# Attention for one query: VectorE's products over K as one nested loop in place of two unrolled ones

## The chip, the cores and the metric

The kernel runs on one core of one Trainium2 chip. Its time is the device time of one execution in microseconds; the median of three runs is given. A profile, taken by the hardware profiler, is of one further execution. The engines are TensorE (PE), VectorE (DVE), ScalarE (ACT), GpSimd (POOL) and SyncE (SP); each has a sequencer of its own that reads the engine's instructions and hands them on (DVEq, ACTq and so on in the profile).

## What is computed

Sixteen heads of attention with a single query row each, over 8192 keys of 256 numbers in bfloat16:

```python
B, H, Sq, Sk, D = 1, 16, 1, 8192, 256
scale = q.shape[-1] ** -0.5
scores = jnp.einsum("bhqd,bhkd->bhqk", q, k) * scale
p = _softmax(scores, axis=-1)
return jnp.einsum("bhqk,bhkd->bhqd", p, v)
```

K and V are 67 MB each and are read once. Each key needs one product with the query and one with its weight, so there is little arithmetic for a byte.

## The kernel before, in words

The heads go in eight pairs. A pair's K (8.4 MB) lies on 128 partitions: 64 for each of its two heads, and on every partition 128 columns (J) of 256 numbers, one key each. V lies in the same way. K has two buffers (the halves of `kbuf`, `par` is the pair's parity), V one, `vbuf`.

SyncE issues all transfers, in the order of `ORDER` (line 17): k0 k1 v0 k2 v1 k3 and so on, with the last K and the last two Vs in pieces. Before K of pair n it waits until the products of pair n - 2 are done (lines 128 to 130): VectorE's share by the semaphore `kd`, GpSimd's by `tp`. Before V it waits until TensorE has used the former V (`pa`, `pr`).

A score is the sum of 256 products of a K column and the query. The 128 columns of a pair are shared out, each half of 64 (a side, `HJ`) apart:
- GpSimd multiplies columns 0 to 23 of the first side and 64 to 81 of the second, three at a time (line 218), and ScalarE adds these up (line 463).
- VectorE takes the others, 24 to 63 and 82 to 127: one `scalar_tensor_tensor` a column (line 262), which multiplies by the scale and the query and adds up into a column of `S`. That is 86 columns a pair, 688 in all.

VectorE's program is a loop over the pairs (line 245). At its start come the former pair's maximum (`top`, line 237), the maximum over partitions (`xmax`, line 241, with a step of TensorE before and after), and the reciprocal of a sum of an older pair. Then VectorE waits for the query and for K (`k_waits`) and runs two loops, one for each side: four times 10 columns for the first, two times 23 for the second (`CH`, line 15; lines 255 to 271). Each pass ends with an increment of `kd`; a pair makes `NC` = 6 of them. Between the two loops stands `half_wait` (line 160), a wait for the second half of K. It holds only in pair 7, whose K comes in two transfers; for the others the semaphore is set ahead.

`ds(...)` takes an offset that is known only at run time. The sequencer works it out with register operations; several that follow each other stand in one instruction, a list, called FUSED_REGOPS in the profile and ISA in the built program. A single one is an ALU_OP (REGISTER_ALU). In the loops of lines 258 to 271 `s` is a plain number, and the offset of a column is (what depends on the pair and the pass) + (a constant). So the list ahead of a column is: add a constant, times 2 (bytes), add the base of `kbuf`; add a constant, times 4, add the base of `S`. That is six operations, each of a register with a constant. The three lists at the start of a pass hold what depends on the loop, with sums of two registers.

After VectorE's and ScalarE's shares come the exponentials on ScalarE (`E`, line 416), then TensorE multiplies V (`doubles`, line 321), after some spare matmuls (line 335) that wait for ScalarE's shares. For the last pair V's last columns go another way (line 391), and VectorE and ScalarE write the end of the result.

## Time and profile before

| | |
|---|---|
| median of 3 runs | 317.76 us (317.5 to 318.17) |
| the profiled execution | 318.02 us, of which the span 316.3 us |
| VectorE busy | 241.9 us (76%) |
| GpSimd busy | 183.8 us (58%) |
| ScalarE busy | 175.0 us (55%) |
| TensorE busy | 127.1 us (40%) |
| HBM read | 134.23 MB, 424 GB/s over the span |

The span runs from the first to the last instruction of the core. Busy time leaves out register, branch and semaphore instructions: those are the sequencer's. A row of the timeline has start, duration, engine, line, operation and tiles, and in brackets the idle time before and what ended it. A row for a line has the engine, the operation, its count, then the shortest, median and longest duration in ns, and the starts of the first and the last. In the chain of waits, a piece is start, duration and what ran.

### The profile page before, as it was taken

Reading aid. Unit: us, or ns where it says so; the run is one execution under the profiler, and the core shown is the slowest. Engines: PE = TensorE matmul, PEld = TensorE weight load, DVE = VectorE, ACT = ScalarE, POOL = GpSimd, SP = SyncE. Lnnn points to the kernel's source line nnn. Section 1 sums busy time; section 2 is a strip of 40 time slices with the busy share of each in tenths; the row PEclk is TensorE's granted clock in tenths of the full one; section 3 lists DMA queues with packets and bytes.
Section 4 is the critical chain, followed back from the end, with each engine's and each line's share of the span. In section 5 each row is a group of like instructions: output and inputs, shape, how many; then the busy total and the mean of one; then the engine's idle time right before and its main releaser. Section 6 shows DMA issues by size and latency. Waiting matters only on the chain.

```text
span 316.3 us, 6771 instructions
## 1 busy us (share of the span) xinstructions
PE 127.1 (40%) x797; PEld 55.0 (17%) x797; DVE 241.9 (76%) x1401; ACT 175.0 (55%) x744; POOL 183.8 (58%) x129
## 2 busy tenths in 40 slices
PE   0000001880092908038710468005790066065686
PEld 0000000240031403014200133002330023022234
DVE  0009997999889997999179990899909998999900
ACT  2005763777477666667237662466625765776531
POOL 3008886488738846885078840888308886588200
PEclk9999999995568766758795597755956559579799
DMA  9999999999999999999999999999999999999995
GB/s 399 398 398 456 472 399 398 514 406 406 398 522 398 406 398 522 398 406 398 522 406 398 439 481 406 398 481 439 406 398 522 406 394 402 478 420 424 434 395 238
DMA packets 3208, 134.26 MB, mean 424 GB/s; under 512 B 358, under 2 KB 390, under 8 KB 646
## 3 DMA queue, kind: packets, MB, share of 16 engines
q1 hardware_dynamic: 3188, 134.23, 98.6%
q8 instruction: 1, 0.02, 0.0%
q10 hardware_dynamic: 18, 0.01, 0.0%
q14 instruction: 1, 0.01, 0.0%
HBM read 134.23 MB, written 0.01 MB: 424 GB/s over the span
## 4 chain that ended last, share of the span: by engine, by line
DMA 67%; PE 21%; DVE 6%; issue 4%; DVEq 1%; SPq 0%; ACT 0%
DMA vbuf<-in_v_dram 60%; PE acc L321 18%; DMA kbuf<-in_k_dram 7%; DVE kbuf L262 5%; PE spare L335 2%; DVEq L262 1%; PE ob L391 0%; DVEq L258 0%; SPq L137 0%; PE mx L296 0%; PE mx L299 0%; PE tot L309 0%; ACT qo L476 0%; DVE small L237 0%; DVE small L241 0%
## 5 line engine op out<-in xcount | busy, mean ns | idle before, releaser
L262 DVE SCALAR_TENSOR_TENSOR kbuf<-kbuf,qrow x688 | 235.7, 417 | 52.3 <-DMA kbuf<-in_k_dram 48.8
L218 POOL TENSOR_TENSOR prod<-kbuf,q_now 128x768 f32 x112 | 181.3, 1641 | 108.9 <-DMA kbuf<-in_k_dram 67.2
L463 ACT ACTIVATE prod<-prod x336 | 135.9, 405 | 102.2 <-POOL prod L218 86.7
L321 PE MATMUL acc<-vbuf,E 128*64 128x512 bf16 x497 | 68.6, 442 | 86.3 <-DMA vbuf<-in_v_dram 86.3
L463 ACT ACTIVATION_READ_ACCUMULATOR prod<-prod x336 | 62.6, 186 | 0.0
L262 DVE DVE_READ_ACCUMULATOR kbuf<-kbuf,qrow x688 | 57.1, 83 | 0.0
L321 PEld LDWEIGHTS acc<-vbuf,E 128*64 128x64 bf16 x497 | 31.6, 127 | 123.3 <-DMA vbuf<-in_v_dram 90.7
L335 PE MATMUL spare<-ident 128*128 128x512 bf16 x120 | 40.9, 507 | 11.1 <-ACT prod L463 8.3
L296 PE MATMUL mx<-ident,small 128*1 128x128 f32 x16 | 3.7, 318 | 83.9 <-DVE small L237 83.8
L335 PEld LDWEIGHTS spare<-ident 128*128 128x128 bf16 x120 | 13.2, 119 | 37.9 <-issue 34.5
L296 PEld LDWEIGHTS mx<-ident,small 128*1 128x1 f32 x16 | 0.7, 81 | 85.1 <-DVE small L237 85.1
L416 ACT ACTIVATE E<-S,negb 64x128 bf16 x16 | 13.8, 863 | 1.6 <-ACT negb L411 1.4
L411 ACT ACTIVATE negb<-mx 128x2 f32<-128x2 f32 x8 | 1.4, 172 | 20.9 <-PE mx L299 20.9
L430 ACT ACTIVATE comb<-acc 98x512 f32<-98x512 f32 x8 | 4.8, 594 | 10.5 <-PE tot L309 10.4
L231 DVE RECIPROCAL small<-tot 34x1 f32 (+1 forms) x8 | 1.3, 160 | 10.9 <-PE tot L309 10.8
L416 ACT ACTIVATION_READ_ACCUMULATOR E<-S,negb 64x1 f32 x16 | 7.9, 492 | 0.0
L346 PE MATMUL ob<-comb,small 98*2 98x128 f32 x64 | 6.2, 326 | 1.0 <-ACT comb L430 0.7
L241 DVE TENSOR_REDUCE small<-mx 1x2 f32<-1x128 f32 x8 | 2.2, 279 | 4.4 <-PE mx L296 4.4
L299 PE MATMUL mx<-small 1*128 1x2 f32 x16 | 3.8, 307 | 3.0 <-DVE small L241 3.0
L437 ACT ACTIVATE qo<-ob,small 2x128 f32 x14 | 4.9, 353 | 0.1
L299 PEld LDWEIGHTS mx<-small 1*128 1x128 f32 x16 | 3.1, 244 | 5.9 <-DVE small L241 5.9
L237 DVE TENSOR_REDUCE small<-S 128x1 f32 x8 | 2.3, 286 | 2.4 <-DVE kbuf L262 2.4
(25 smaller groups left out, 21.0 us busy)
## 6 DMA issues: line engine op xcount, KB each, us to landing
vbuf<-in_v_dram SPq DMA_DIRECT2D x2, 4480.0 KB, 19.5
kbuf<-in_k_dram SPq DMA_DIRECT2D x2, 4096.0 KB, 42.1
vbuf<-in_v_dram SPq DMA_DIRECT2D x1, 3712.0 KB, 29.6
vbuf<-in_v_dram SPq DMA_DIRECT2D x1, 1792.0 KB, 9.9
vbuf<-in_v_dram SPq DMA_DIRECT2D x1, 1024.0 KB, 12.1
vbuf<-in_v_dram SPq DMA_DIRECT2D x1, 640.0 KB, 13.1
vbuf<-in_v_dram SPq DMA_DIRECT2D x1, 256.0 KB, 13.3
kbuf<-in_k_dram SPq DMA_DIRECT2D x7, 41.3
```

Of the source, the lines that this page charges most:

```text
L218: pool.tensor_tensor(out=prod[:, b * GRP * D : (b + 1) * GRP * D].rearrange("p (b d) -> p b d", b=GRP), in0=kbuf[:, ds(par * (J * D) + i * ...
L237: dve.tensor_reduce(m[:, :], S[:, ds(i % 2 * J, J)], AX.X, ALU.max).then_inc(sem("m"), 1)
L262: ins = dve.scalar_tensor_tensor(out=col, in0=col, scalar=SCALE, in1=qrow[:, ds(par * 512, D)], op0=ALU.mult, op1=ALU.mult, accum_out=S[:, ...
L296: pe.matmul(mx[0:1, 0:P], lhsT=m[:, :], rhs=ident[:, :], start=True, stop=True).then_inc(sem("mT"), 1)
L299: pe.matmul(sm, lhsT=ones[0:1, :].to_broadcast([1, P]), rhs=g[:, :], start=True, stop=True,).then_inc(sem("bc"), 1)
L321: ins = pe.matmul(acc[at : at + STRIP, :], lhsT=E[:, x : x + STRIP], rhs=vbuf[:, j * D : (j + 2) * D], start=(j < 4), stop=(j >= J - 4), s ...
L335: pe.matmul(spare[:, :].rearrange("p (b x) -> p b x", x=2 * P), lhsT=flat[:, n * P : (n + 1) * P], rhs=flat.rearrange("p (b x) -> p b x", ...
L346: ins = pe.matmul(ob[row : row + 2, 0:HW], lhsT=sel[:, 2 * n : 2 * n + 2], rhs=comb[:, n * D + a : n * D + a + HW], start=(n == 0), stop=( ...
L416: ins = act.activation(out=E[rows, 0 : 2 * J].rearrange("p (b two i t) -> p b i two t", b=J // BLK, two=2, t=2)[:, :, :, :, x], in_=S[rows ...
L430: act.activation(out=comb[:, :], in_=acc[0:ROWS, :], func=ACT.Copy).then_inc(sem("cm"), 1)
L437: ins = act.activation(out=qo[:, ds(i * D + a, HW)], in_=ob[row : row + 2, 0:HW], func=ACT.Copy, scale=recip[row : row + 2, ds(i, 1)],)
L463: ins = act.activation(out=part, in_=part, func=ACT.Copy, scale=SCALE, accum_out=S[:, ds(first + b, 1)],)
```

## The change

VectorE's two loops become one loop over the sides with a loop of five passes of 8 columns in it. Both sides then have 40 columns in the loops (24 to 63 and 82 to 121); the 6 columns that the second side has more (122 to 127) stand once behind them. `half_wait` stands at the end of each side, so also behind the second one. `kd` gets 2 x 5 + 1 = 11 increments a pair; the waits on it use `NC` and `(n - 1) * NC` and so follow. The same 86 columns are worked through in the same order. Nothing else in the kernel is changed.

```diff
-CH = (10, 23)
+CH = 8
...
-    SC = [(HJ - n) // c for n, c in zip(NPL, CH)]
-    NG, NC = sum(SG), sum(SC)
+    SC = (HJ - NPL[0]) // CH
+    REST = NPL[0] - NPL[1]
+    NG, NC = sum(SG), SIDES * SC + 1
...
-                    for s in range(SIDES):
-                        if s:
-                            half_wait(dve, count)
-                        with dve.Fori(0, SC[s]) as c:
-                            for b in range(CH[s]):
-                                j = s * HJ + NPL[s] + b
-                                col = kbuf[:, ds(par * (J * D) + c * (CH[s] * D) + j * D, D)]
-                                ins = dve.scalar_tensor_tensor(
...
-                                    accum_out=S[:, ds(par * J + c * CH[s] + j, 1)],
-                                )
+
+                    def column(j):
+                        col = kbuf[:, ds(par * (J * D) + j * D, D)]
+                        return dve.scalar_tensor_tensor(
...
+                            accum_out=S[:, ds(par * J + j, 1)],
+                        )
+
+                    with dve.Fori(0, SIDES) as s:
+                        with dve.Fori(0, SC) as c:
+                            for b in range(CH):
+                                ins = column(s * (HJ - REST) + c * CH + (NPL[0] + b))
                             ins.then_inc(sem("kd"), 1)
+                        half_wait(dve, count)
+                    for j in range(J - REST, J):
+                        ins = column(j)
+                    ins.then_inc(sem("kd"), 1)
```

In the new loop the column's number `j` comes from two loops' registers, and `ds` gets `par * (J * D) + j * D`. The list ahead of a column becomes: add a constant (this is `j`), times 256, add the pair's part (register to register), times 2, add the base of `kbuf`; add `j` to the pair's part of `S` (register to register), times 4. That is seven operations; the eighth, the base of `S`, stands behind the list as a single REGISTER_ALU. For the 6 columns behind the loops `j` is a plain number, and their lists are as before.

On VectorE, from the last wait for K to the second column, before (ISA is a list, SCALAR_TENSOR_TENSOR a column):

```order
L258 UNCONDITIONAL_BRANCH [waits k1]
L258 ISA
L262 ISA x2
L262 SCALAR_TENSOR_TENSOR kbuf,S<-kbuf,qrow 128x256
L262 ISA
L262 SCALAR_TENSOR_TENSOR kbuf,S<-kbuf,qrow 128x256
```

and now, in lines of the new kernel (L269 the outer loop, L270 the inner one, L259 the column):

```order
L269 UNCONDITIONAL_BRANCH [waits k1]
L270 UNCONDITIONAL_BRANCH
L270 ISA
L259 ISA x2
L259 SCALAR_TENSOR_TENSOR kbuf,S<-kbuf,qrow 128x256
L259 ISA
L259 REGISTER_ALU
L259 SCALAR_TENSOR_TENSOR kbuf,S<-kbuf,qrow 128x256
```

Each pass still begins with three lists, and from the second column on a REGISTER_ALU stands between the list and the column.

On VectorE, from the end of the first side's last pass to the next column, before:

```order
L258 REGISTER_ALU
L258 COMPARE_AND_BRANCH
L160 ISA
L258 UNCONDITIONAL_BRANCH [waits kb]
L258 ISA
L262 ISA x2
L262 SCALAR_TENSOR_TENSOR kbuf,S<-kbuf,qrow 128x256
```

and now, where the row behind L269 is the first of the 6 single columns (between the sides the branch goes back to the start of the inner loop instead):

```order
L270 REGISTER_ALU
L270 COMPARE_AND_BRANCH
L161 ISA
L269 REGISTER_ALU [waits kb]
L269 COMPARE_AND_BRANCH
L259 ISA x2
L259 SCALAR_TENSOR_TENSOR kbuf,S<-kbuf,qrow 128x256
```

The outer loop's own count and branch have come between the wait for the half and the next column.

## Prediction

> **What bounds the kernel now.** I read the page's slices and chain first, then VectorE's group with its idle time, then its timeline, and last its sequencer.

> ```profile
> DMA  9999999999999999999999999999999999999995
> q1 hardware_dynamic: 3188, 134.23, 98.6%
> DMA 67%; PE 21%; DVE 6%; issue 4%; DVEq 1%; SPq 0%; ACT 0%
> L262 DVE SCALAR_TENSOR_TENSOR kbuf<-kbuf,qrow x688 | 235.7, 417 | 52.3 <-DMA kbuf<-in_k_dram 48.8
> ```

> The transfers bound it: 134.23 MB, with the sixteen engines busy for 98.6% of the span. VectorE has slack: 688 products, and 48.8 us of waiting for K. So a faster VectorE gains nothing, and a slower one costs nothing until its slack is gone. How much slack there is, the timeline of VectorE's waits and the table by stretch tell (after the stretch's bounds come its length, then busy us and count of PE, PEld, DVE, ACT, POOL).

> ```profile
> 23.64 0.42 DVE L262 SCALAR_TENSOR_TENSOR kbuf<-kbuf,qrow  x1 [23.64 <-DMA kbuf<-in_k_dram]
> 160.03 0.42 DVE L262 SCALAR_TENSOR_TENSOR kbuf<-kbuf,qrow  x1 [7.92 <-DMA kbuf<-in_k_dram]
> 198.65 0.42 DVE L262 SCALAR_TENSOR_TENSOR kbuf<-kbuf,qrow  x1 [7.63 <-DMA kbuf<-in_k_dram]
> 237.50 0.42 DVE L262 SCALAR_TENSOR_TENSOR kbuf<-kbuf,qrow  x1 [7.88 <-DMA kbuf<-in_k_dram]
> 266.55 0.41 DVE L262 SCALAR_TENSOR_TENSOR kbuf<-kbuf,qrow  x1
> 269.63 0.42 DVE L262 SCALAR_TENSOR_TENSOR kbuf<-kbuf,qrow  x1 [1.15 <-issue]
> 299.40 0.29 DVE L237 TENSOR_REDUCE small<-S 128x1 f32 x1 [0.30 <-DVE kbuf L262]
> 160.00:189.50 29.50, 8.71 (x66) 4.29 (x66) 29.47 (x172) 19.50 (x87) 22.53 (x14) 0.71 1.06 458
> ```

> K lands every 38.6 to 38.9 us in the steady part (160.03, 198.65, 237.50). VectorE works 29.47 us of that (86 products, so 342 ns for each), needs 2.67 us from the last product of a pair to the first of the next when nothing holds it (266.96 to 269.63), and waits the rest, some 7 us. So its period may grow from 32.1 to 38.8 us before it sets the pace. The slack at the very end is smaller: pair 6 starts when its K lands (237.50), pair 7 follows at once, and VectorE is done at 299.10, shortly before the last V.

> **What feeds VectorE.** The change touches no product; it touches what its sequencer does between two. The chain of waits at the start of pair 0 shows the sequencer alone (DVEq), since VectorE stands empty there; each piece is an instruction and the "issue" before it the gap.

> ```profile
> 23.00 0.25 DVEq L258
> 23.25 0.03 issue
> 23.29 0.17 DVEq L262
> 23.46 0.03 issue
> 23.49 0.10 DVEq L262
> 24.53 0.09 DVEq L262
> 24.93 0.09 DVEq L262
> 25.32 0.09 DVEq L262
> 25.59 0.06 DVEq L258
> 26.27 0.08 DVEq L262
> L262 DVEq FUSED_REGOPS  x736: 82/93/179, 23.3 to 296.7; - x184
> L258 DVEq FUSED_REGOPS  x48: 241/241/249, 23.0 to 289.6; - x48
> L258 DVEq ALU_OP  x48: 40/40/47, 25.5 to 297.1; - x48
> ```

> From 24.53 to 25.32 the sequencer prepares four columns, one each 198 ns: the list of register operations 93, the product's own issue and gaps 105. VectorE takes 342, so now the sequencer runs ahead, and the turn of the loop hides in that lead. The turn: the product of the list at 25.32 is out at 25.52, the three lists that follow the branch end with the one at 26.27, and that product is out 0.08 + 0.105 later, at 26.46: 0.94 us from product to product.

> **Part 1: the address of a column.** Now a column's list holds six operations, each with a constant: the part that depends on the loop was summed before. In the new loop the column number is itself a sum of two loops' registers, so the list has seven operations, two of which add a register to a register, and an ALU_OP for the eighth. Such mixed lists stand in this trace. On VectorE: the third row above (0.17, median 179; six operations, one mixed) and the first (0.25, median 241; seven, two mixed, one a modulo). On ScalarE the list nearest to the new one, seven operations of which two are mixed and one a division, and then the plain lists of six:

> ```profile
> L463 ACTq FUSED_REGOPS  x2: 144/171/198, 101.1 to 101.2; - x2
> L463 ACTq FUSED_REGOPS  x2: 74/76/79, 101.5 to 101.7; - x2
> L237 DVEq FUSED_REGOPS  x8: 115/115/121, 53.3 to 299.2; - x8
> ```

> The 198 is that mixed list; the 144 is a plain one of six with two modulos, so a modulo or division is some 35 there, and the mixed list without it 162, against 76 plain. VectorE's sequencer takes 93 for a plain six, 1.22 as much: 199. From VectorE's own row: 241 less a modulo. L237's list, four operations with a modulo, takes 115 where the plain list of four (the 82 in the row x736) has none, so a modulo is 33, and the list 208. I take **202 ns**. The ends: 179, the shorter mixed list, and 241, the longer one.

> [...]

> Column: 198 - 93 + 202, and the ALU_OP 40 with a gap of 0.03: **0.379 us**. That is more than the 0.342 of the product, so VectorE now waits for its sequencer at each column, no lead builds up, and each loop turn shows in full. That is the step on which all hangs.

> **Part 2: the turns.** Inner turn: 0.94, with the list behind the first one mixed now as before but of seven, 202 for 179: **0.96 us**. There are four inner turns on a side. At a side's end, the wait for the second half of K stands between two loops, and now also behind the second. Today's rows at that place, first loop's end to second loop's list:

> ```profile
> 35.45 0.05 DVEq L258
> 35.54 0.11 DVEq L160
> 35.79 0.04 DVEq L258
> 35.86 0.16 DVEq L258
> L258 DVEq ALU_OP  x1: 40/40/40, 35.4 to 35.4; - x1
> ```

> ALU_OP 0.07, a branch not taken 0.09, list 0.16, wait 0.09, MOVE 0.07. New, between the sides: this without the MOVE (0.42), the outer ALU_OP 0.07, its taken branch 0.20 (the list at 26.27 has 0.179 and 0.241 and two gaps of 0.03 before it, so the first begins at 25.79, and the branch at 25.59), two MOVEs 0.14, the three lists and the issue 0.70: **1.53 us**. Behind the second side: 0.42, 0.07, branch not taken 0.09, two plain lists and the issue 0.36: **0.94 us**. The waits themselves cost nothing: the half is there except in pair 7, where VectorE reaches the wait later than today. The six last columns have constant offsets, so plain lists, and run at 0.342.

> **The sum.** One pair, first product to last: 70 steps in the loops at 0.379 = 26.5; 8 turns at 0.96 = 7.7; 1.53; 0.94; 5 steps at 0.342 = 1.7. That is 38.4, and with the last product's 0.42 it is 38.8 us, against 29.47. Between pairs 2.67, with two more MOVEs and the longer list 2.85. The period is 41.7 us, over the 38.8 that K needs: **VectorE sets the pace**, the transfers get pauses. Start at 23.64 + 0.16 = 23.8; eight pairs 310.5; seven gaps 20.0: VectorE ends at 354.3. Transfers don't interfere: K for pair n+2 is issued when pair n is done, and has 41.7 us for itself and one V, 39 us of transfer. The new count of kd (11 for 6) reaches its total at the same last column.

> The tail, from the rows of TensorE and the output:

> ```profile
> 302.11 2.48 PE L335 MATMUL spare<-ident 128*128 128x512 bf16 x8 [0.51 <-issue]
> 305.38 4.07 PE L321 MATMUL acc<-vbuf,E 128*64 128x512 bf16 x35 [0.79 <-DMA vbuf<-in_v_dram]
> 309.67 1.70 PE L321 MATMUL acc<-vbuf,E 128*64 128x512 bf16 x14 [0.22 <-DMA vbuf<-in_v_dram]
> 56.57 6.39 PE L335 MATMUL spare<-ident 128*128 128x512 bf16 x16 [1.03 <-issue]
> 315.17 0.28 SPq L149 DMA_DIRECT2D out_dram<-qo  x1
> ```

> From VectorE's end (299.10) to the span's (316.3) it is 17.2 us, of which 1.0 (0.79 and 0.22) waited for V, which will long be there. TensorE comes to it after a rest, as at 56.57, where a spare matmul took 0.40 (16 in 6.39) for 0.31 (8 in 2.48): 0.7 more for the 8, and a little behind them. So 17.2 again: span 371.5, and with the 1.7 that lie around the span (318.02 for 316.3) 373.2 us. The profiled run lies 0.26 above the median of 317.76, which I don't take off; with 1 us for the branches that the next part bounds, the forecast is **374 us**.

> **Ends.** With lists of 179: 23 ns less over 560 steps, 360. With 241, in the columns and the turns: 398. The turn's branch may cost 0.30 as in today's long loop, not 0.20 as in its short one:

> ```profile
> L258 DVEq COMPARE_BRANCH  x1: 56/56/56, 289.3 to 289.3; - x1
> L258 DVEq FUSED_REGOPS  x1: 241/241/241, 289.6 to 289.6; - x1
> ```

> The new loop's body is nearer to the short one in length; some 70 turns would add 7: 380.

> **Rivals.**
> 1. *Not slower: the sequencer stays hidden.* Mechanism: the sequencer prepares eight columns and their turn within eight products, 2.73 us, and VectorE never starves. With a turn of 0.96 that decides at 0.25 us a column. For it: today a column takes 0.198, and all turns are hidden. Against: the mixed rows on two engines, and the ALU_OP alone brings it to 0.27. Time: as now, 317.8. [...] 4%.
> 2. *Partly hidden.* A mixed list costs only a plain one (some 105 ns), or the gaps of 0.03 belong to the recording and are absent in timed runs: 0.28 for a column either way, hidden; only turns show, about 1.7 us a pair at 31.1 us. K still sets the pace up to pair 6; pairs 6 and 7 in sequence end 3.6 us late, at 302.7, of which the tail hides 1.0: about 321. Against: the mixed lists above, 162 to 241 ns, none near a plain one; for the gaps no row speaks either way. 11%.
> 3. *Faster*: a shorter program that starts or loads sooner. VectorE waits 23.64 us for its first K anyway. 1%.

> **How the numbers follow.** The forecast has 84%, nearly all of it in 358 to 390 (ends 360 and 398, the longer branch 380); with that range no more than 2 in 10 is left out. Rival 2 is slower too. A measurement here can tell 0.2% (0.6 us) from no change: slower 0.95, same 0.04, faster 0.01.

> **What would show it.** Right: VectorE's busy time unchanged near 236 us but its products 0.38 us apart in the loops; the median of the lists at L259 near 202 ns; VectorE's waits for K near zero after pair 0 and "issue" in their place; DMA slices with gaps; VectorE's end near 354. Wrong: products 0.342 apart inside the eight, or waits of 7 us for K still there.

## The result, and the profile after

The changed kernel takes 371.88 us (median of 6 runs, 371.42 to 372.28), the one before 318.22 us (6 runs beside them, 317.5 to 319.54). The ratio is 1.168, with a 95% interval of 1.166 to 1.171. The forecast was 374, with a range of 358 to 390.

From the page of the changed kernel: the slices of the transfers, their queue, the chain that ended last, the product's group, and K's issue with the time to its landing.

```profile
DMA  8999998899988998989989898998979995009920
q1 hardware_dynamic: 3188, 134.23, 85.3%
DVE 46%; issue 19%; DVEq 19%; DMA 12%; PE 5%; ACT 0%; SPq 0%
L259 DVE SCALAR_TENSOR_TENSOR kbuf<-kbuf,qrow x688 | 260.2, 421 | 80.4 <-issue 79.4
kbuf<-in_k_dram SPq DMA_DIRECT2D x7, 21.8
```

The same bytes now fill 85.3% of the engines' span in place of 98.6%, and the slices have gaps. The chain has changed hands: the transfers had 67% of it, now VectorE, its sequencer and "issue" have 84%. VectorE's idle time is put down to "issue" now (79.4 us of 80.4, of which 23.9 are pair 0's wait for its first K, a wait for several semaphores), that is to nothing that the profile shows. K lands 21.8 us after its issue, where it was 41.3: it is now issued some 25.5 us after the V ahead of it (at 145.62 us after 120.07, for instance), and V lands 25.5 us after its own issue, so hardly any of it is left to queue behind.

VectorE's timeline shows where it loses. The rows are starts and durations of the product in one pass of 8, then the start of the next pass (27.47); then the start of pair 6 (273.15), a later turn in it (286.48 to 287.42), the last column of its first side and the first of its second (290.04 and 291.54), the last column of its second side and the first of the six behind it (308.39 and 309.49), the start of pair 7 (314.65), and the reduction that follows the last product of all.

```profile
24.27 0.42 DVE L259 SCALAR_TENSOR_TENSOR kbuf<-kbuf,qrow  x1
24.64 0.42 DVE L259 SCALAR_TENSOR_TENSOR kbuf<-kbuf,qrow  x1
25.01 0.42 DVE L259 SCALAR_TENSOR_TENSOR kbuf<-kbuf,qrow  x1
...
26.51 0.42 DVE L259 SCALAR_TENSOR_TENSOR kbuf<-kbuf,qrow  x1
27.47 0.42 DVE L259 SCALAR_TENSOR_TENSOR kbuf<-kbuf,qrow  x1 [0.53 <-issue]
...
273.15 0.42 DVE L259 SCALAR_TENSOR_TENSOR kbuf<-kbuf,qrow  x1 [1.31 <-issue]
...
286.48 0.42 DVE L259 SCALAR_TENSOR_TENSOR kbuf<-kbuf,qrow  x1
287.42 0.42 DVE L259 SCALAR_TENSOR_TENSOR kbuf<-kbuf,qrow  x1 [0.51 <-issue]
...
290.04 0.42 DVE L259 SCALAR_TENSOR_TENSOR kbuf<-kbuf,qrow  x1
291.54 0.42 DVE L259 SCALAR_TENSOR_TENSOR kbuf<-kbuf,qrow  x1 [1.08 <-DMA kbuf<-in_k_dram]
...
308.39 0.42 DVE L259 SCALAR_TENSOR_TENSOR kbuf<-kbuf,qrow  x1
309.49 0.42 DVE L259 SCALAR_TENSOR_TENSOR kbuf<-kbuf,qrow  x1 [0.67 <-issue]
...
314.65 0.42 DVE L259 SCALAR_TENSOR_TENSOR kbuf<-kbuf,qrow  x1 [1.31 <-issue]
353.43 0.29 DVE L238 TENSOR_REDUCE small<-S 128x1 f32 x1 [0.30 <-DVE kbuf L259]
```

Inside a pass the products start 0.374 us apart (six steps from 24.27 to 26.51), from pass to pass 0.96 at the first turn of a pair and 0.93 to 0.96 at the others, between the sides 1.50 and behind the second side 1.10. (The DMA named at 291.54 is no wait for K: the step is 1.50 or 1.51 in all eight pairs.) There is almost no idle time inside a pass in these rows, though VectorE could start a product each 0.342: a product reads as 0.42 busy, and back to back its last part overlaps the next one. So the starving hardly shows as idle time. It shows in the distance of the starts, and in a busy time that grew with the same work (the group from 235.7 to 260.2). From the start of a pair to that of the next it is 41.5 us, and there is no wait for K between pairs any more: the gap is 2.96 to 3.04 us each time.

What the sequencer does in that time, by lines: the lists at the column and the single operation behind them (L259), and the lists at the start of a pass (L270).

```profile
L259 DVEq FUSED_REGOPS  x776: 75/198/204, 23.5 to 351.8; - x194
L259 DVEq ALU_OP  x560: 40/40/40, 24.2 to 349.8; - x187
L270 DVEq FUSED_REGOPS  x80: 234/234/249, 23.2 to 346.7; - x80
```

A list takes 198 ns, where the plain one took 93, and there are 560 ALU_OPs that were not there.

The tail, TensorE's rows and the last transfer:

```profile
356.34 3.57 PE L341 MATMUL spare<-ident 128*128 128x512 bf16 x8
359.85 5.88 PE L327 MATMUL acc<-vbuf,E 128*64 128x512 bf16 x49
366.88 1.85 PE L397 MATMUL ob<-vbuf,E 128*2 128x128 bf16 x60
369.15 0.28 SPq L150 DMA_DIRECT2D out_dram<-qo  x1
```

V is long there: the 49 matmuls run in one piece. The spare ones take 3.57 where they took 2.48, 634 ns each for 379 (the medians). They come after 18.5 us without a matmul and a few short ones, and the granted clock is 0.50 over them, where it was 1.00 in the kernel before. The granted clock alone doesn't explain it: at 56.57 in the kernel before, after a rest of 50.9 us, the median was 631 ns with 1.00 granted. From VectorE's last product (353.1) to the end of the span (370.3) it is 17.2 us.

### The profile page after: what moved, and what is told of

It reads as the page before. It is cut to its first block, busy times and chain, and to the rows that moved or that the text cites. A ratio compares the mean times of both kernels' runs of the same rounds, so it can differ in the third digit from the quotient of the medians.

```text
span 370.3 us, 7539 instructions
## 1 busy us (share of the span) xinstructions
PE 116.9 (32%) x797; PEld 52.8 (14%) x797; DVE 267.0 (72%) x1401; ACT 174.6 (47%) x744; POOL 183.7 (50%) x129
## 3 DMA queue, kind: packets, MB, share of 16 engines
q1 hardware_dynamic: 3188, 134.23, 85.3%
HBM read 134.23 MB, written 0.01 MB: 363 GB/s over the span
## 4 chain that ended last, share of the span: by engine, by line
DVE 46%; issue 19%; DVEq 19%; DMA 12%; PE 5%; ACT 0%; SPq 0%
DVE kbuf L259 45%; DVEq L259 12%; DMA kbuf<-in_k_dram 12%; DVEq L270 4%; PE acc L327 2%; PE mx L302 1%; PE spare L341 1%; DVEq L269 1%; DVE small L238 1%; DVEq L161 0%; PE ob L397 0%; DVEq L157 0%; PE ob L352 0%; DVEq L238 0%; DVE small L242 0%
## 5 line engine op out<-in xcount | busy, mean ns | idle before, releaser
L259 DVE SCALAR_TENSOR_TENSOR kbuf<-kbuf,qrow x688 | 260.2, 421 | 80.4 <-issue 79.4
L302 PE MATMUL mx<-ident,small 128*1 128x128 f32 x16 | 4.7, 394 | 236.1 <-DVE small L238 236.1
L259 DVE DVE_READ_ACCUMULATOR kbuf<-kbuf,qrow x688 | 56.8, 83 | 0.0
L327 PE MATMUL acc<-vbuf,E 128*64 128x512 bf16 x497 | 55.6, 381 | 0.0
L341 PE MATMUL spare<-ident 128*128 128x512 bf16 x120 | 41.3, 516 | 9.4 <-ACT prod L469 8.2
L327 PEld LDWEIGHTS acc<-vbuf,E 128*64 128x64 bf16 x497 | 28.0, 110 | 27.6 <-issue 4.1
L352 PE MATMUL ob<-comb,small 98*2 98x128 f32 x64 | 7.7, 391 | 0.7 <-ACT comb L436 0.7
L305 PE MATMUL mx<-small 1*128 1x2 f32 x16 | 4.7, 358 | 3.0 <-DVE small L242 3.0
L305 PEld LDWEIGHTS mx<-small 1*128 1x128 f32 x16 | 4.0, 306 | 7.0 <-DVE small L242 7.0
## 6 DMA issues: line engine op xcount, KB each, us to landing
vbuf<-in_v_dram SPq DMA_DIRECT2D x1, 1024.0 KB, 16.6
kbuf<-in_k_dram SPq DMA_DIRECT2D x7, 21.8
```

Of the source, the lines that this page charges most:

```text
L259: return dve.scalar_tensor_tensor(out=col, in0=col, scalar=SCALE, in1=qrow[:, ds(par * 512, D)], op0=ALU.mult, op1=ALU.mult, accum_out=S[: ...
L302: pe.matmul(mx[0:1, 0:P], lhsT=m[:, :], rhs=ident[:, :], start=True, stop=True).then_inc(sem("mT"), 1)
L305: pe.matmul(sm, lhsT=ones[0:1, :].to_broadcast([1, P]), rhs=g[:, :], start=True, stop=True,).then_inc(sem("bc"), 1)
L327: ins = pe.matmul(acc[at : at + STRIP, :], lhsT=E[:, x : x + STRIP], rhs=vbuf[:, j * D : (j + 2) * D], start=(j < 4), stop=(j >= J - 4), s ...
L341: pe.matmul(spare[:, :].rearrange("p (b x) -> p b x", x=2 * P), lhsT=flat[:, n * P : (n + 1) * P], rhs=flat.rearrange("p (b x) -> p b x", ...
L352: ins = pe.matmul(ob[row : row + 2, 0:HW], lhsT=sel[:, 2 * n : 2 * n + 2], rhs=comb[:, n * D + a : n * D + a + HW], start=(n == 0), stop=( ...
```

## The experiments

The theory: what counts is the time that the sequencer needs for a column and for a turn, and the mixed lists raise it over the product's 0.342 us. Rival A: the turns cost, with 80 in place of 48, or the nesting. Rival B: the loop over the sides costs, with the wait at its end. Each kernel was timed in turn with the kernel before (317.88 and 317.89 in the two groups).

**The nested loop with plain lists.** Only the way in which the offsets are written is changed; loops, turns, wait and the six columns behind are those of the changed kernel.

```diff
-def column(j):
-col = kbuf[:, ds(par * (J * D) + j * D, D)]
+def column(j, s=0, c=0):
+col = kbuf[:, ds(par * (J * D) + s * ((HJ - REST) * D) + c * (CH * D) + j * D, D)]
...
-accum_out=S[:, ds(par * J + j, 1)],
+accum_out=S[:, ds(par * J + s * (HJ - REST) + c * CH + j, 1)],
...
-ins = column(s * (HJ - REST) + c * CH + (NPL[0] + b))
+ins = column(NPL[0] + b, s, c)
```

> The new nested loop of five passes with 8 columns, with the same turns and the same wait behind each side, but the offsets written as a sum over pair, side and pass plus a constant, so that each column's list is six operations with constants and no ALU_OP stands behind it. Theory (the mixed lists starve VectorE): a column takes the sequencer about 0.20 us, VectorE runs at 0.342 a product again and hides the inner turns; about 29.8 us a pair, time within 1 us of the kernel before (318.2). Rival A (the turns and the nesting cost, whatever the lists): 371, as the changed kernel. Rival B (the loop over the sides with the wait in it costs): 371 as well.

Measured: 317.75 us, ratio 0.998 (0.996 to 1.001). The lists, with the least, median and greatest duration in ns:

```profile
L259 DVEq FUSED_REGOPS  x856: 59/93/179, 23.5 to 297.1; - x172
```

On the timeline, the starts of pair 6 and of the reduction behind pair 7:

```profile
237.38 0.42 DVE L259 SCALAR_TENSOR_TENSOR kbuf<-kbuf,qrow  x1 [7.87 <-issue]
299.60 0.29 DVE L238 TENSOR_REDUCE small<-S 128x1 f32 x1 [0.30 <-DVE kbuf L259]
```

The median list is 93 ns again, VectorE is idle for some 8 us before pair 6 again and is done at 299.3. The whole loss is gone with the mixed lists, and the turns, the nesting and the wait are hidden. Rivals A and B fall. (The 7.87 before pair 6 is put down to "issue" here, as a wait for several semaphores; the start falls on 237.4, where K landed in the kernel before, at 237.50.)

**The two unrolled loops with mixed lists**, the opposite: the loops of the kernel before, the offsets of the new one.

```diff
-j = s * HJ + NPL[s] + b
-col = kbuf[:, ds(par * (J * D) + c * (CH[s] * D) + j * D, D)]
+j = c * CH[s] + (s * HJ + NPL[s] + b)
+col = kbuf[:, ds(par * (J * D) + j * D, D)]
...
-accum_out=S[:, ds(par * J + c * CH[s] + j, 1)],
+accum_out=S[:, ds(par * J + j, 1)],
```

> The two unrolled loops of 10 and 23 columns of the kernel before, six passes a pair and one wait between them, but with the column's number as a register, so that each list is the changed kernel's mixed one with an ALU_OP behind it. Theory: 80 steps of 0.374 and 4 turns of 0.94 and one of 1.2 make 35.3 us a pair; with 2.8 between pairs 38.1, just under the 38.8 that K needs, so K sets the pace up to pair 6, and pairs 6 and 7 in sequence end at about 311: 330 in all. Rivals A and B (turns, nesting, wait): 318, as the kernel before, since none of these is changed.

Measured: 346.39 us, ratio 1.088 (1.083 to 1.094). The lists:

```profile
L262 DVEq FUSED_REGOPS  x736: 64/198/198, 23.3 to 326.9; - x184
```

On the timeline, the start of pair 6 and what follows the last product:

```profile
254.12 0.42 DVE L262 SCALAR_TENSOR_TENSOR kbuf<-kbuf,qrow  x1 [1.11 <-issue]
327.54 0.08 DVE L262 DVE_READ_ACCUMULATOR kbuf<-kbuf,qrow  x1
```

The loss comes with the lists alone, in the old loops. But the size was missed by 16 us. The pair takes what was expected (35.2 for 35.3), yet pair 6 starts at 254.1, behind pair 5, and not at 237.4, where K lets it start in the kernel before. The expectation held VectorE to K's pace as long as its period stays below 38.8. That is wrong: VectorE starts pair 1 after pair 0, at 62 here, so with a long pair it falls behind K from the beginning, and catches up only as far as its period is shorter than K's. In the kernel before, pairs 1 and 2 don't wait for K, and pair 3 hardly does; the starts of pairs 2 and 3 there:

```profile
88.23 0.42 DVE L262 SCALAR_TENSOR_TENSOR kbuf<-kbuf,qrow  x1 [1.15 <-issue]
121.13 0.42 DVE L262 SCALAR_TENSOR_TENSOR kbuf<-kbuf,qrow  x1 [1.72 <-DMA kbuf<-in_k_dram]
```

**The nested loop with passes of 20.** The edit is CH = 20 in place of 8.

> The changed kernel with CH = 20, so two passes a side in place of five; lists mixed as in the changed kernel. Theory: 76 steps of 0.374, 2 inner turns of 0.95, 1.53 between the sides, 0.94 and 1.7 behind them: 34.9 us a pair, K sets the pace up to pair 6, end of VectorE about 310, time 329. Rival A (all of the extra 54 us are the 80 turns, 0.67 us each): 32 turns are left of 80, and VectorE needs some 33 us a pair, 322 to 324. Rival B (the loop over the sides): 371.

Measured: 349.56 us, ratio 1.099 (1.094 to 1.104). Rival A's 322 to 324 and rival B's 371 are both missed; so is the theory's 329, for the same reason as above: 24.0 + 8 pairs of 35.71 + 7 gaps of 3.02 give 330.8 for VectorE's end, and with the tail of 17.2 and the 1.7 around the span 349.7. The starts of pairs 6 and 7:

```profile
256.45 0.42 DVE L259 SCALAR_TENSOR_TENSOR kbuf<-kbuf,qrow  x1 [1.31 <-issue]
295.14 0.42 DVE L259 SCALAR_TENSOR_TENSOR kbuf<-kbuf,qrow  x1 [1.32 <-issue]
```

A pair was 0.75 us longer than expected: 0.5 of that is a longer step in the middle of each of the four passes (the last section has a row), the rest mostly the turns, 1.02 to 1.05 for 0.95.

**Plain lists with passes of 4.** The edit is CH = 4 in the first experiment's kernel.

> As the nested loop with plain lists, but with CH = 4: ten passes a side, 20 turns a pair. It asks when turns alone starve VectorE. Theory (a pass costs what its sequencer needs): 3 columns at 0.198 and a turn of 1.12 (one list more than in the changed kernel) are 1.71 us for four products of 0.342, 1.37; a pair takes about 36.9 us, the period with 2.85 is 39.7, just over K's 38.8; VectorE ends at about 339, time 358. If turns were hidden however short the pass: 318.

Measured: 360.18 us, ratio 1.131 (1.126 to 1.137). Products of two passes:

```profile
24.65 0.41 DVE L259 SCALAR_TENSOR_TENSOR kbuf<-kbuf,qrow  x1
24.99 0.41 DVE L259 SCALAR_TENSOR_TENSOR kbuf<-kbuf,qrow  x1
25.72 0.42 DVE L259 SCALAR_TENSOR_TENSOR kbuf<-kbuf,qrow  x1 [0.30 <-issue]
...
26.75 0.42 DVE L259 SCALAR_TENSOR_TENSOR kbuf<-kbuf,qrow  x1
27.43 0.42 DVE L259 SCALAR_TENSOR_TENSOR kbuf<-kbuf,qrow  x1 [0.26 <-issue]
```

Inside the pass the products stand 0.34 apart, so the plain lists keep up, and at each turn VectorE waits. A pass takes 1.71 us (25.72 to 27.43), as worked out. So a turn is free only if the pass is long enough to have gained its time: with 8 columns and plain lists it was (317.75 us), with 4 it is not.

**The short plain version.** The pair's part is put into the column's number, so both offsets are one register and constants.

```diff
-col = kbuf[:, ds(par * (J * D) + j * D, D)]
+col = kbuf[:, ds(j * D, D)]
...
-accum_out=S[:, ds(par * J + j, 1)],
+accum_out=S[:, ds(j, 1)],
...
-ins = column(s * (HJ - REST) + c * CH + (NPL[0] + b))
+ins = column(par * J + s * (HJ - REST) + c * CH + (NPL[0] + b))
...
-ins = column(j)
+ins = column(par * J + j)
```

> The new nested loop, five passes of 8, with the pair's part put into the column's number: both offsets come from one register plus a constant, so each list is again six operations with constants, and the lists at the start of a pass are shorter than in the plain version before. Theory: VectorE back to 29.5 us a pair, time within 0.2% of the kernel before. If the nesting itself cost anything: 0.2 us or more a turn would show as over 2 us in all.

Measured: 317.64 us, ratio 0.999 (0.997 to 1.001). The lists:

```profile
L259 DVEq FUSED_REGOPS  x776: 65/93/142, 23.5 to 296.6; - x194
```

The nested loop with its shorter program costs nothing that this measurement can tell if its offsets are written so.

**The kernel before with idle sequencer work.** Plain lists and the old loops; behind each column two increments of semaphores on which nobody waits.

```diff
+for z in range(2):
+    dve.nop().then_inc(sem(f"z{b % 8}{z}"), 1)
```

> The kernel before, with its plain lists, and behind each column two semaphore increments that nobody waits for: they are the sequencer's alone, some 0.097 us each with the gap. It asks whether the time of the sequencer for a column is what counts, or something in the mixed lists. Theory: 80 steps of 0.392, 4 turns of 1.13 and one of 1.4 make 37.7 us a pair, with 3.1 between pairs VectorE ends at 347, time 366. If only the register sums mattered: 318.

Measured: 373.83 us, ratio 1.174 (1.169 to 1.179). The increments on the sequencer:

```profile
L272 DVEq EVENT_SEMAPHORE  x1376: 21/21/21, 23.6 to 355.1; - x197
```

Three products in a row on the timeline:

```profile
24.78 0.42 DVE L262 SCALAR_TENSOR_TENSOR kbuf<-kbuf,qrow  x1
25.17 0.42 DVE L262 SCALAR_TENSOR_TENSOR kbuf<-kbuf,qrow  x1
25.55 0.42 DVE L262 SCALAR_TENSOR_TENSOR kbuf<-kbuf,qrow  x1
```

The lists are plain, and a column takes 0.385 us. So it is the sequencer's time for a column that counts, also when increments fill it and not register sums. The expectation was 8 us low: the pair took 38.3 for 37.7, with turns of some 1.22 in the loop of 10 for 1.13 and of 1.35 in the loop of 23, and a longer step in each pass of 10 (see the last section), and 3.6 from pair to pair for 3.1. Much of the latter is VectorE's sequencer again: the reduction starts 1.00 us after a pair's last product, where it was 0.30 in the kernel before. The last increments and the loop's end stand ahead of it, with no lead to hide them:

```profile
356.28 0.28 DVE L237 TENSOR_REDUCE small<-S 128x1 f32 x1 [1.00 <-DVE kbuf L262]
```

**Half mixed.** The offset into kbuf plain, that into S with one register sum; six operations in the list, and the ALU_OP. The edit is shown against the first experiment's kernel.

```diff
 col = kbuf[:, ds(par * (J * D) + s * ((HJ - REST) * D) + c * (CH * D) + j * D, D)]
...
-accum_out=S[:, ds(par * J + s * (HJ - REST) + c * CH + j, 1)],
+accum_out=S[:, ds(par * J + (s * (HJ - REST) + c * CH + j), 1)],
```

> The nested loop with the offset into kbuf as in the plain version, and the offset into S with the pair's part added to a register: a list of six with one register sum, and the ALU_OP behind it. Theory: list 0.179 (as VectorE's row of that shape before), 0.356 for a column, turns of 1.04; 37.9 us a pair, 367. If the cost were per register sum, so that one sum is half of two: a list of some 0.145 and 0.32 for a column, 35.2 us a pair, 346.

Measured: 366.20 us, ratio 1.150 (1.145 to 1.155), beside the theory's 367 and not the rival's 346. The lists:

```profile
L259 DVEq FUSED_REGOPS  x776: 93/173/217, 23.6 to 346.8; - x194
```

Three products in a row on the timeline:

```profile
24.78 0.42 DVE L259 SCALAR_TENSOR_TENSOR kbuf<-kbuf,qrow  x1
25.12 0.42 DVE L259 SCALAR_TENSOR_TENSOR kbuf<-kbuf,qrow  x1
25.47 0.42 DVE L259 SCALAR_TENSOR_TENSOR kbuf<-kbuf,qrow  x1
```

One register sum makes a list of six 173 ns and not 93; the second sum and a seventh operation add only 25 more. It is the first one that costs. A column takes 0.349 here, hardly over the product's time, so nearly all of this loss is that no lead builds up and the turns show in full.

**The short plain version with passes of 4**, for the range between (CH = 4).

> As the short plain version with CH = 4, ten passes a side. It is made for the range between, where VectorE loses a little: pass 3 columns at 0.198 and a turn of 0.84, 1.43 us for 1.37 of products; 31.5 us a pair. Theory: K still holds VectorE back up to pair 6 (start at 237.4), then pairs 6 and 7 follow each other, end at 303.3 for 300.1 that the tail hides: 321. If a slower VectorE showed in full from the first pair on: 8 times 2 us more, 334. If only a period over 38.8 us cost: 318.

Measured: 321.13 us, ratio 1.009 (1.006 to 1.012). Starts of pairs 6 and 7, and the reduction behind pair 7:

```profile
236.47 0.42 DVE L259 SCALAR_TENSOR_TENSOR kbuf<-kbuf,qrow  x1 [5.55 <-issue]
270.87 0.42 DVE L259 SCALAR_TENSOR_TENSOR kbuf<-kbuf,qrow  x1 [1.20 <-issue]
302.76 0.28 DVE L238 TENSOR_REDUCE small<-S 128x1 f32 x1 [0.30 <-DVE kbuf L259]
```

A pair of 31.6 us has caught up with K by pair 6: VectorE is idle for 5.55 us before it, where 1.20 is idle without a wait for K. Only pairs 6 and 7 show, 2.1 us each, less the 1.0 by which pair 6 starts earlier than in the kernel before (236.47 for 237.50). The expectation had that 1 us from the tail, which would no longer wait for V. V is there, but the spare matmuls take 3.57 us again, after a rest of only 3.1 us, and the tail stays 17.2.

With this the missed expectations fall in place. VectorE's end is the later of two: start 23.9 + 8 pairs + 7 gaps, or K's landing at 237 + 2 pairs + a gap. The time is the end + 17.2 + 1.7 (the tails of the slower kernels are 16.6 to 17.5). With pair and gap read from each trace, so as an account and not as a test, it gives 346.5 for the two loops with mixed lists (327.6 + 18.9), 360.4 for plain passes of 4, 321.4 for the short ones.

## Why the prediction was right

The mechanism and its place were right: VectorE starves because its sequencer needs longer than 0.342 us for a column. The two opposite exchanges of lists and loops show that this is the lists' doing, and the idle increments that other work of the sequencer does the same. Term by term:

| step of the prediction | worked out | measured |
|---|---|---|
| list of seven with two register sums | 0.202 us | 0.198 |
| column | 0.379 | 0.374 |
| turn from pass to pass | 0.96 | 0.94 (286.48 to 287.42); the first of a pair 0.96 |
| between the sides | 1.53 | 1.50 (290.04 to 291.54) |
| behind the second side | 0.94 | 1.10 (308.39 to 309.49) |
| one pair | 38.8 | 38.5 |
| from pair to pair | 2.85 | 3.03 |
| VectorE's end | 354.3 | 353.1 |
| from there to the span's end | 17.2 | 17.2 |
| sum, with 1.7 around the span | 373.2 | 371.99 in the profiled run |

The price of the list was taken from lists on two engines that did the same kind of arithmetic. The ratio between the two sequencers that the plain lists of six gave, 93 to 76 ns or 1.22, held for the mixed ones: 198 ns here, and on ScalarE a similar list with its division estimated away (from the rows of 198, 144 and 76 ns before) 162, again 1.22. The 1 us put in for longer branches did not come: the turn is as with the short branch, 0.20 us from it to the list (26.64 to 26.84). The 0.16 missed behind the second side is 1.5 us over eight pairs (in pair 0 the step is 1.37), the gaps between pairs came 1.2 longer in all; the shorter column gives back 2.8 and the shorter turns 0.9. The tail's 17.2 is in part luck: the spare matmuls cost 1.1 us more where 0.7 was put in, and the last sixty took 1.85 for 2.22. At 56.57, where the 0.7 came from, the sixteen spare ones take 0.40 us each on average; the eight of the tail take 0.45.

Two things in the text were wrong, though the number does not rest on them.
- "So its period may grow from 32.1 to 38.8 us before it sets the pace." The two loops with mixed lists have a period of 38.4 and lose 28 us. VectorE has the waits for K from pair 3 on to use up, and no more; by the two ends above, it sets the pace from a pair of some 32.5 us on, a period of some 35.5. With the changed kernel's pair of 38.5 us that made no difference. Made into expectations for two experiments, the step missed them by 16 and 21 us, of which some 6 in the second are the longer pair's.
- "VectorE's busy time unchanged near 236 us" as a mark of being right: it is 260.2 with the same products, because products of 0.42 that start 0.374 apart overlap less than those that start 0.342 apart.

Whether the recording itself lengthens the sequencer's gaps, a thought in rival 2, stays open: no run here is known to be without it.

## What to carry to other kernels

An engine with short instructions needs its sequencer to be faster than itself: for products of 0.342 us, plain lists at 0.198 us a column cost nothing in passes of 8, and 0.374 or 0.385 us a column cost 28 to 56 us. Add up the register operations, single ones, branches and semaphore steps between two instructions and compare with the distance of their starts, pass by pass with the loop's turn included. Write an offset in a loop as (everything that depends on registers) + (a constant), so that the sum of registers is made once a pass; here that is all the difference between 317.6 and 371.9 us, with the same loops. And an engine that waits in every round has only those waits as its slack, beginning where they begin; a period below that of the transfers is not enough if the engine starts behind them (38.4 us for 38.8 lost 28 us here).

## What the runs showed of the hardware that was not expected

```profile
27.35 0.42 DVE L259 SCALAR_TENSOR_TENSOR kbuf<-kbuf,qrow  x1
28.13 0.42 DVE L259 SCALAR_TENSOR_TENSOR kbuf<-kbuf,qrow  x1 [0.35 <-issue]
```

0.78 us here in the first pass and 0.49 to 0.51 in later ones, for 0.374; in the kernel with the idle increments the eighth step of each pass of 10, 0.79 in the first and 0.49 to 0.52 in later ones, for 0.385. The changed kernel and the loops of 23 columns have no such step, also the one of 23 in the kernel with the increments, so the length of the body alone does not make it. The cause stays open.
